# 32x32 block turns on VectorE in place of TensorE transposes, for q and k of two batches and for the late normalised tokens

## The chip, the cores and the metric

The kernel runs on one core of one Trainium2 chip. The metric is the device time of one execution in microseconds (us). Before the change three runs gave a median of 906.98 us, from 904.29 to 907.66.

## The reference

Inputs are float32: q, k and v of shape (4 batches, 8 heads, 768 tokens, 64), a decay per head, and two weights of 512x2048 and 2048x512. First comes causal linear attention with decay, in blocks of the sequence:

```python
intra = einsum('bhij,bhjd->bhid', einsum('bhic,bhjc->bhij', qb, kb) * Dmask, vb)
inter = einsum('bhid,bhde->bhie', qb * lam_pow, kv_state)
out[block] = intra + inter
kv_state = lam_block * kv_state + einsum('bhsd,bhse->bhde', kb * rev_pow, vb)
```

The heads are put side by side into x of (4, 768, 512). Then a Fourier mixing layer with a channel MLP:

```python
u = x + real(fft(fft(x, axis=1), axis=2))
un = (u - mean(u)) / sqrt(var(u) + 1e-6)
out = u + maximum(un @ w_ch1, 0) @ w_ch2
```

Scores need q and k with the head dimension on partitions, and the MLP needs un with the 512 features on partitions. Both arrive with tokens on partitions, so both are transposed.

## The kernel before, in words

**Attention.** A batch b is cut into 6 chunks of 128 tokens (`attn_chunk`). A chunk loads k, q and v, all heads, with tokens on partitions (L261, on SP's queue). TensorE transposes two heads at a time into PSUM (L272 for k, L277 for q, four 128x128 each) and ScalarE copies the result to kT and qT (L274, L279). VectorE scales q into qs (L282), reading it from PSUM. Scores (L290) are masked by the decay on VectorE (L294). The state is updated (L305), the output is summed from state and scores (L318, L322), copied (L325), transposed back (L329) and copied to x (L332, L333). Tokens are also stored to two DRAM arrays xa and xb (L336 to L340, on ScalarE's queue), from which the FFT gathers tokens in mirrored order (L377, L380, L385, on GpSimd's queue).

**Fourier layer.** `fft_ln` folds each batch by its symmetries on VectorE (L365 to L368, L405 to L416), so that the sequence transform is 20 matmuls (L440); the width transform (L453 to L458) follows, and VectorE adds the result to x (L509 to L513). `norm(g)` works on groups of two tiles of 128 tokens: statistics (L470), the factor (L474 and L475 on GpSimd), the normalised tokens un (L482), four TensorE transposes a tile (L486), a ScalarE copy into ut (L487).

**MLP, plain and late.** There are 12 groups (batch, g). The first four are PLAIN: their MLP runs as written (L545, rectified by ScalarE at L553 and VectorE at L551; L559, added and stored at L565, L566). The other eight are LATE: ut is stored to DRAM as utd (L494), u as ud (L497). Two late groups at a time are then multiplied with a seven-product scheme for 2x2 blocks (L627, L674). This needs sums and differences of weight blocks (`combine_weights`, L604) and of the two groups (us, ur, L617 to L620); `load_u` (L611) reads utd back.

**Weights.** 32 raw loads of 512 KB (L227) are converted on VectorE and ScalarE (L232 to L240) in the first 190 us.

**Order.** Each stage is a generator that yields an estimated duration. `weave` interleaves a lead with another generator in a given ratio: weight conversion under the first attention batches, then the plain groups' MLP as fill under the attention and Fourier stages of batches 1 to 3, and what is left of it under `combine_weights`. The Tile scheduler may then move instructions ahead of one another by its own estimates; only those marked `keep_in_program_order` stay. On each engine the instructions then run in a fixed order. Tiles come from pools: a new tile waits until the readers of the one whose buffer it takes have finished. When attention and Fourier stages end, their pools are closed, and the late stage's tiles lie over the same memory.

Of the kernel before, what the change touches and what calls it, by code (L numbers as in the profile page):

```python
# [10 lines left out]
F32 = mybir.dt.float32  # L11
# [64 lines left out]
def kernel(  # L76
# [10 lines left out]
    nc = tc.nc  # L87
    B, H, S, D = q.shape
    DM = H * D
    DFF = moe_w_ch1.shape[1]  # L90
    C = 128
    NC = S // C
    HC = NC // 2
    HP = H // 2
    NK = S // 4 + 1
    KO = DM // 128
# [5 lines left out]
    G = 2  # L102
# [18 lines left out]
    ld = front_pool("ld", 2)  # L121
    at = front_pool("at", 1)
    xn = front_pool("xn", HC)
    fp = front_pool("fp", 1)
# [13 lines left out]
    def new(pool, shape, tag, **kw):  # L138
        cnt[0] += 1
        return pool.tile(shape, F32, tag=tag, name=f"{tag}{cnt[0]}", **kw)  # L140

    def psum_a(shape):
        return new(pa, shape, "pa")
# [12 lines left out]
    n, b2 = 1, 0  # L156
# [45 lines left out]
    def row_of(j, n=128):  # L202
        return bass.IndirectOffsetOnAxis(ap=ix[0:n, j:j + 1], axis=0)
# [45 lines left out]
            yield 1.0  # L249


    xs, xn_, xd = {}, {}, {}

    def pair(t, hp):
        return t[:, 2 * hp:2 * hp + 2, :].rearrange("p a d -> p (a d)")

    def attn_chunk(b, c):
        rows = slice(c * C, (c + 1) * C)
        kt, qt, vt = (new(ld, [C, H, D], nm) for nm in ("k", "q", "v"))
        for t, src in ((kt, k), (qt, q), (vt, v)):  # L260
            nc.sync.dma_start(t, src[b, :, rows, :].rearrange("h p d -> p h d"))  # L261
        if b == 0:
            load_tables(c)

        last = c == NC - 1
        if not last:
            kd = new(at, [C, H, D], "kd")
            nc.gpsimd.tensor_tensor(kd, kt, kpow, op=ALU.mult)

        ptk = psum_a([128, HP, C])  # L270
        for hp in range(HP):
            nc.tensor.transpose(ptk[:, hp, :], pair(kt, hp), ident)  # L272
        kT = new(at, [128, HP, C], "kT", bufs=2)
        nc.scalar.copy(kT, ptk)  # L274
        ptq = psum_a([128, HP, C])
        for hp in range(HP):
            nc.tensor.transpose(ptq[:, hp, :], pair(qt, hp), ident)  # L277
        qT = new(at, [128, HP, C], "qT", bufs=2)
        nc.scalar.copy(qT, ptq)  # L279
        if c > 0:  # L280
            qs = new(at, [128, HP, C], "qs")
            nc.vector.tensor_tensor(qs, ptq, qpow, op=ALU.mult)  # L282
        yield 1.2


        mm = nc.tensor.matmul
        pss = [psum_a([C, HP, C]) for _ in range(2)]
        for hp in range(HP):
            for hi in range(2):
                mm(pss[hi][:, hp, :], lhsT=kT[HD[hi], hp, :], rhs=qT[HD[hi], hp, :], start=True, stop=True)  # L290
        sc = []
        for hi in range(2):
            t = new(at, [C, HP, C], "sc", bufs=3)
            nc.vector.tensor_tensor(t, pss[hi], decay[:, hi::2, :], op=ALU.mult)  # L294
            sc.append(t)
        yield 1.5


        s_old, s_new = st[(c + 1) % 2], st[c % 2]
        if not last:  # L300
            pu = psum_a([128, HP, D])
            for hp in range(HP):
                for hi in range(2):
                    h = 2 * hp + hi
                    mm(pu[HD[hi], hp, :], lhsT=kd[:, h, :], rhs=vt[:, h, :], start=True, stop=True)  # L305
            if c == 0:
                nc.vector.tensor_copy(s_new, pu)
            else:
                nc.gpsimd.tensor_tensor(s_new, s_old, spow.broadcast_to([128, HP, D]), op=ALU.mult)
                nc.vector.tensor_tensor(s_new, s_new, pu, op=ALU.add)  # L310
            yield 0.9


        po = psum_a([128, HP, C])
        if c > 0:
            for hp in range(HP):
                for hi in range(2):
                    mm(po[HD[hi], hp, :], lhsT=s_old[HD[hi], hp, :], rhs=qs[HD[hi], hp, :],  # L318
                       start=(hp == 0), stop=False, skip_group_check=True)
        for hp in range(HP):  # L320
            for hi in range(2):
                mm(po[HD[hi], hp, :], lhsT=vt[:, 2 * hp + hi, :], rhs=sc[hi][:, hp, :],  # L322
                   start=(c == 0 and hp == 0), stop=(hp == HP - 1), skip_group_check=True)
        oT = new(at, [128, HP, C], "oT")
        nc.scalar.copy(oT, po)  # L325
        yield 2.0
        px = psum_a([C, HP, 128])
        for hp in range(HP):
            nc.tensor.transpose(px[:, hp, :], oT[:, hp, :], ident)  # L329
        px = px.rearrange("p h e -> p (h e)")  # L330
        x = xn_[b, c] = new(xp, [C, DM], "x") if c < HC else new(xn, [C, DM], "xn")
        nc.scalar.copy(x[:, 0:HM], px[:, 0:HM])  # L332
        nc.scalar.copy(x[:, HM:DM], px[:, DM - 1:HM - 1:-1])  # L333
        if c == 0:
            xd[b] = (dram.tile([S - 256, DM], F32, name=f"xa{b}"), dram.tile([257, DM], F32, name=f"xb{b}"))
            nc.scalar.dma_start(xd[b][1][256:257], x[0:1])  # L336
        elif c < NC - 1:
            nc.scalar.dma_start(xd[b][0][(c - 1) * C:c * C], x)
        if c >= NC - 2:
            nc.scalar.dma_start(xd[b][1][(c - NC + 2) * C:(c - NC + 3) * C], x)  # L340
        if c == NC - 2:
            mirror_a(b)
        elif c == NC - 1:
            mirror_b(b)
        yield 1.7
# [9 lines left out]
        nc.gpsimd.memset(t, 0.0)  # L355

    gather = nc.gpsimd.indirect_dma_start
    eo, r1s = {}, {}

    def fold_x(b, a, n, i, lo, hi):  # L360

        e, o = eo[b][a]
        tt = nc.vector.tensor_tensor

        tc.keep_in_program_order(tt(e[0:n, i, 0:DM], lo, hi, op=ALU.add))  # L365
        tc.keep_in_program_order(tt(o[0:n, i, 0:DM], lo, hi, op=ALU.subtract))
        tt(e[0:n, i, 1:HM], e[0:n, i, 1:HM], e[0:n, i, HM:DM - 1], op=ALU.add)
        tt(o[0:n, i, 1:HM], o[0:n, i, 1:HM], o[0:n, i, HM:DM - 1], op=ALU.subtract)  # L368

    def mirror_a(b):  # L370

        xa = xd[b][0]
        r1 = r1s[b] = [new(fp, [128, DM], f"r{a}") for a in range(2)]

        eo[b] = [(new(fp, [128, 2, 2 * W], f"fe{a}"), new(fp, [128, 2, 2 * W], f"fo{a}")) for a in range(2)]
        for a, n in enumerate(BLK):
            gather(out=r1[a][0:n], out_offset=None, in_=xa[:, :], in_offset=row_of(a, n))  # L377
        for t in range(2, HC):
            u = xs[b, HC + t] = new(xp, [128, DM], "x")
            gather(out=u[:, :], out_offset=None, in_=xa[:, :], in_offset=row_of(2 + t))  # L380
# [6 lines left out]
            xs[b, t] = xn_.pop((b, t))  # L387

    def fold_a(b):
        r1 = r1s.pop(b)  # L390
        for a, n in enumerate(BLK):
            fold_x(b, a, n, 1, r1[a][0:n], xn_[b, HC + a][0:n])

    def fold_b(b):

# [31 lines left out]
    def fft_ln(b):  # L427
# [38 lines left out]
        def norm(g):  # L466
            mv = new(np_, [128, G, 2], "mv")
            for i in range(G):
                stt = new(np_, [128, 6], "stt")
                nc.vector.bn_stats(stt, xs[b, TT[g][i]])  # L470
                nc.vector.bn_aggr(mv[:, i, :], stt)
            ve = new(np_, [128, G], "ve")
            rs = new(np_, [128, G], "rs")
            nc.gpsimd.tensor_scalar(ve, mv[:, :, 1], EPS, None, op0=ALU.add)  # L474
            nc.gpsimd.tensor_tensor(rs, ve, mhalf, op=ALU.pow)  # L475
            yield 1.0
            ut = new(up, [128, KO, G * 128], "ut")
            for i in range(G):
                un = new(np_, [128, DM], "un", bufs=1)
                u = xs[b, TT[g][i]]  # L480
                for o, x in ((un[:, 0:HM], u[:, 0:HM]), (un[:, HM:DM], u[:, DM - 1:HM - 1:-1])):
                    nc.vector.tensor_scalar(o, x, mv[:, i, 0:1], rs[:, i:i + 1],  # L482
                                            op0=ALU.subtract, op1=ALU.mult)
                pt = psum_a([128, KO, 128])
                for c in range(KO):
                    nc.tensor.transpose(pt[:, c, :], un[:, 128 * c:128 * c + 128], ident)  # L486
                nc.scalar.copy(ut[:, :, 128 * i:128 * i + 128], pt)  # L487
                yield 0.7
            if (b, g) in PLAIN:
                uts[b, g] = ut  # L490
                return

            utd[b, g] = dram.tile([128, KO, G * 128], F32, name=f"utd{b}{g}")
            nc.sync.dma_start(utd[b, g], ut)  # L494
            for T in TT[g]:
                ud[b, T] = dram.tile([128, DM], F32, name=f"ud{b}{T}")
                nc.sync.dma_start(ud[b, T], xs.pop((b, T)))  # L497
# [309 lines left out]
```

## Time and profile before

| | |
|---|---|
| median of 3 runs | 906.98 us (904.29 to 907.66) |
| the profiled execution | 908.43 us, its span 906.4 us |
| mean granted TensorE clock | 0.975 |
| PE busy | 826.5 us, 91% |
| DVE busy | 437.0 us, 48% |
| ACT busy | 209.0 us, 23% |
| POOL busy | 90.7 us, 10% |
| DMA packets | 96190, 72.43 MB, 77536 of them under 512 B |
| k, q, v loads (256 KB each) to landing | 3.8, 3.9, 3.2 us |
| utd stores (512 KB each) to landing | 3.3 us |
| ud stores (256 KB each) to landing | 2.1 us |

PE is TensorE's matmuls, PEld its weight loads, DVE is VectorE, ACT ScalarE, POOL GpSimd, SP the engine that issues most DMAs. In a group's line stand source line, engine, operation, output<-input by name, shapes and count; then the busy time in us and the mean ns of one; then the idle time of the engine just before them and what ended it. A line of the timeline begins with the start and the duration in us; "x4" are so many instructions of one kind in a row. Matmuls are pipelined, so a group's mean ns is longer than the time until the next can start. The slices of the page are 40 equal parts of the span (22.7 us each), with the busy share in tenths.

### The profile page before, as it was taken

Reading aid. Unit: us, or ns where it says so; the run is one execution under the profiler, and the core shown is the slowest. Engines: PE = TensorE matmul, PEld = TensorE weight load, DVE = VectorE, ACT = ScalarE, POOL = GpSimd, SP = SyncE. Lnnn points to the kernel's source line nnn. Section 1 sums busy time; section 2 is a strip of 40 time slices with the busy share of each in tenths; the row PEclk is TensorE's granted clock in tenths of the full one; section 3 lists DMA queues with packets and bytes.
Section 4 is the critical chain, followed back from the end, with each engine's and each line's share of the span. In section 5 each row is a group of like instructions: output and inputs, shape, how many; then the busy total and the mean of one; then the engine's idle time right before and its main releaser. Section 6 shows DMA issues by size and latency. Waiting matters only on the chain.

```text
span 906.4 us, 11761 instructions
## 1 busy us (share of the span) xinstructions
PE 826.5 (91%) x4660; PEld 652.9 (72%) x4660; DVE 437.0 (48%) x1006; ACT 209.0 (23%) x467; POOL 90.7 (10%) x108
## 2 busy tenths in 40 slices
PE   4775678699999999999999899999999999999997
PEld 2564566545865578567874588888888888888886
DVE  4779869854532135443567756115531454135410
ACT  3665436620211212223221021002200120012100
POOL 2214211100010110012200100000000000000000
PEclk9988789899999999999999999999999999999999
DMA  9899316611013241344216001110011100110010
GB/s 230 232 249 252 111 52 179 209 39 35 24 47 93 74 120 47 116 141 129 88 47 215 29 1 47 46 35 12 1 59 47 35 1 1 47 47 1 0 35 24
DMA packets 96190, 72.43 MB, mean 80 GB/s; under 512 B 77536, under 2 KB 79080, under 8 KB 96136
## 3 DMA queue, kind: packets, MB, share of 16 engines
q1 hardware_dynamic: 90176, 57.51, 22.3%
q0 software_dynamic: 2496, 7.87, 2.7%
q10 hardware_dynamic: 3464, 6.30, 2.0%
q8 instruction: 37, 0.61, 0.3%
q14 instruction: 17, 0.14, 0.0%
HBM read 50.68 MB, written 20.99 MB: 79 GB/s over the span
## 4 chain that ended last, share of the span: by engine, by line
PE 51%; DVE 5%; issue 1%; DMA 1%; POOL 1%; ACT 0%; POOLq 0%; DVEq 0%; ACTq 0%
PE p L627 21%; PE p L674 21%; PE pm L545 1%; PE pm L559 1%; PE pa L440 1%; PE pa L486 1%; PE pa L290 1%; PE pa L322 1%; DVE stt L470 1%; DVE w1s L604 1%; DVE w2s L604 1%; PE pa L318 1%; POOL rs L475 0%; DVE x L512 0%; DVE x L513 0%
## 5 line engine op out<-in xcount | busy, mean ns | idle before, releaser
L545 PE MATMUL pm<-ut,w 128*128 128x256 f32 x512 | 124.2, 392 | 10.0 <-ACT hr L553 8.2
L559 PE MATMUL pm<-w,hr 128*128 128x512 f32 x256 | 120.6, 602 | 0.0
L545 PEld LDWEIGHTS pm<-ut,w 128*128 128x128 f32 x512 | 95.9, 194 | 26.3 <-ACT hr L553 8.9
L627 PE MATMUL p<-ur,w 128*128 128x256 f32 x384 | 95.1, 382 | 3.3 <-DVE ur L620 1.9
L627 PEld LDWEIGHTS p<-ur,w 128*128 128x128 f32 x384 | 73.3, 191 | 14.5 <-issue 2.3
L559 PEld LDWEIGHTS pm<-w,hr 128*128 128x128 f32 x256 | 44.8, 190 | 40.3 <-issue 38.8
L627 PE MATMUL p<-us,w1s 128*128 128x256 f32 x256 | 66.6, 383 | 0.0
L674 PE MATMUL p<-w,hs 128*128 128x256 f32 x256 | 58.0, 379 | 0.5 <-DVE y L695 0.5
L674 PE MATMUL p<-w2s,hs 128*128 128x256 f32 x256 | 57.9, 379 | 0.0
L674 PE MATMUL p<-w,ha 128*128 128x256 f32 x256 | 57.9, 379 | 0.0
L535 POOL DMA_INDIRECT out_dram<-y,ix x12 | 13.3, 1109 | 409.9 <-DVE y L698 370.9
L627 PEld LDWEIGHTS p<-us,w1s 128*128 128x128 f32 x256 | 49.2, 192 | 6.9
L674 PEld LDWEIGHTS p<-w,hs 128*128 128x128 f32 x256 | 48.5, 190 | 7.5 <-DVE y L695 0.9
L674 PEld LDWEIGHTS p<-w2s,hs 128*128 128x128 f32 x256 | 48.6, 190 | 6.6
L674 PEld LDWEIGHTS p<-w,ha 128*128 128x128 f32 x256 | 48.6, 190 | 6.6
L290 PEld LDWEIGHTS pa<-qT,kT 64*128 64x128 f32 x384 | 30.1, 193 | 25.9 <-ACT qT L279 14.4
L654 ACT COPY ha<-p 128x256 f32<-128x256 f32 x32 | 11.9, 372 | 155.6 <-PE p L627 155.5
L290 PE MATMUL pa<-qT,kT 64*128 64x128 f32 x384 | 36.2, 291 | 11.7 <-ACT qT L279 10.0
L294 DVE TENSOR_TENSOR sc<-pa,decay 128x512 f32<-128x512 f32 x48 | 31.8, 684 | 29.1 <-PE pa L290 26.3
L322 PE MATMUL pa<-sc,v 128*64 128x128 f32 x384 | 31.2, 290 | 9.8 <-DVE sc L294 9.8
L665 DVE TENSOR_TENSOR ha<-p,ha 128x256 f32<-128x256 f32 x32 | 13.6, 425 | 47.1 <-ACT ha L664 47.1
L322 PEld LDWEIGHTS pa<-sc,v 128*64 128x64 f32 x384 | 23.4, 143 | 17.5 <-DVE sc L294 13.4
(141 smaller groups left out, 1188.3 us busy)
## 6 DMA issues: line engine op xcount, KB each, us to landing
raw<-in_moe_w_ch_dram SPq DMA_DIRECT2D x32, 512.0 KB, 5.2
k<-in_k_dram SPq DMA_DIRECT2D x24, 256.0 KB, 3.8
q<-in_q_dram SPq DMA_DIRECT2D x24, 256.0 KB, 3.9
v<-in_v_dram SPq DMA_DIRECT2D x24, 256.0 KB, 3.2
ud<-x SPq DMA_DIRECT2D x16, 256.0 KB, 2.1
utd<-ut SPq DMA_DIRECT2D x8, 512.0 KB, 3.3
u<-ud SPq DMA_DIRECT2D x16, 256.0 KB, 2.6
ur<-utd SPq DMA_DIRECT2D x8, 512.0 KB, 5.6
```

The lines of the kernel that those rows point to most:

```text
L290: mm(pss[hi][:, hp, :], lhsT=kT[HD[hi], hp, :], rhs=qT[HD[hi], hp, :], start=True, stop=True)
L294: nc.vector.tensor_tensor(t, pss[hi], decay[:, hi::2, :], op=ALU.mult)
L318: mm(po[HD[hi], hp, :], lhsT=s_old[HD[hi], hp, :], rhs=qs[HD[hi], hp, :], start=(hp == 0), stop=False, skip_group_check=True)
L322: mm(po[HD[hi], hp, :], lhsT=vt[:, 2 * hp + hi, :], rhs=sc[hi][:, hp, :], start=(c == 0 and hp == 0), stop=(hp == HP - 1), skip_group_chec ...
L535: nc.gpsimd.indirect_dma_start(out=out.rearrange("b s d -> (b s) d"), out_offset=row_of(2 + HC * (b + 1) + T - HC), in_=y[:, :], in_offset ...
L545: nc.tensor.matmul(ps, lhsT=w1[:, c, 128 * fc:128 * fc + 128], rhs=ut[:, c, :], start=(c == 0), stop=(c == KO - 1))
L559: nc.tensor.matmul(ps, lhsT=hr[fc // 4][:, fc % 4, 128 * i:128 * i + 128], rhs=w2[:, fc, :], start=(fc == 0), stop=(fc == FO - 1))
L604: V.tensor_tensor(o[:, i:i + n // 2], x[:, i:i + n // 2], y[:, i:i + n // 2], op=op)
L627: nc.tensor.matmul(ps, lhsT=s2.A[a][:, kt, 128 * i:128 * i + 128], rhs=U[b][:, kt, :], start=(first and kt == 0), stop=(kt == 1), skip_gro ...
L654: nc.scalar.copy(a11, two(X))
L665: V.tensor_tensor(a22, two(Z), a22, op=ADD)
L674: nc.tensor.matmul(ps, lhsT=h[a][:, s, i, :], rhs=s2.B[b][:, i, :], start=(first and i == 0), stop=(i == HF - 1), skip_group_check=True)
```

## The change

Four things change; line numbers in the diff's new code differ from those above.

1. For batches 2 and 3, kT and qT no longer come from TensorE. Every second chunk, `turned` fills a tile for two chunks (kb or qb, one buffer each) with 16 DMAs. A DMA takes 32 of a head's 64 dimensions for 256 tokens and puts 32x32 blocks where they belong after a transpose, each still unturned: 32 partitions, 8 runs of 32 elements (128 B) each. VectorE's transpose, which turns each 32x32 block in place, then makes kT or qT of a chunk from it. k with tokens on partitions is still loaded for the state, except in the last chunk. qs reads qT in SBUF.
2. For batches 0 and 1, q is loaded into the memory of qb and kb by turns.
3. For late groups, un is turned in 32x32 blocks by VectorE into uq (one buffer), and four DMAs a tile write the blocks to their places in utd, in runs of 128 B. The plain groups keep TensorE's transposes.
4. The first gather of a batch lands in a half of the tile fo, and the fold works on it in place; the tiles r0 and r1 are gone.

```diff
+        def turned(nm, load, src):
+            if c % 2 == 0:
+                t = qk[load] = new(ld, [128, HP, 2 * C], load, bufs=1)
+                for a in range(4):
+                    for hp in range(HP):
+                        nc.sync.dma_start(t[32 * a:32 * a + 32, hp].rearrange("n (t d) -> n t d", d=32),
+                                          src[b, 2 * hp + a // 2, c * C:(c + 2) * C, 32 * (a % 2):32 * (a % 2) + 32]
+                                          .rearrange("(t n) d -> n t d", n=32))
+            tT = new(at, [128, HP, C], nm, bufs=2)
+            nc.vector.transpose(tT, qk[load][:, :, c % 2 * C:(c % 2 + 1) * C])
+            return tT
+
+        blocks = b >= 2
+        if blocks:
+            kT, qT = turned("kT", "kb", k), turned("qT", "qb", q)
+            ptq = qT
+            if not last:
+                kt = natural("k", k)
+        else:
+            kt, qt = natural("k", k), new(ld, [128, HP, 2 * C], "kb" if c % 2 else "qb", bufs=1)
...
-        r1 = r1s[b] = [new(fp, [128, DM], f"r{a}") for a in range(2)]
-            gather(out=r1[a][0:n], out_offset=None, in_=xa[:, :], in_offset=row_of(a, n))
+            gather(out=eo[b][a][1][0:n, 1, 0:DM], out_offset=None, in_=xa[:, :], in_offset=row_of(a, n))
...
-                pt = psum_a([128, KO, 128])
-                for c in range(KO):
-                    nc.tensor.transpose(pt[:, c, :], un[:, 128 * c:128 * c + 128], ident)
-                nc.scalar.copy(ut[:, :, 128 * i:128 * i + 128], pt)
+                if plain:
...
+                else:
+                    uq = new(np_, [128, DM], "uq", bufs=1)
+                    nc.vector.transpose(uq, un)
+                    for r in range(0, 128, 32):
+                        dst = to[:, :, 128 * i + r:128 * i + r + 32].rearrange("(a d) c n -> d c a n", d=32)
+                        src = uq[r:r + 32].rearrange("p (c a n) -> p c a n", c=KO, n=32)
+                        nc.sync.dma_start(dst, src)
...
-            nc.sync.dma_start(utd[b, g], ut)
```

More of the change, by code (lines that the diff above doesn't have):

```diff
@@ L249, in weights @@
             yield 1.0
-    xs, xn_, xd = {}, {}, {}
+    xs, xn_, xd, qk = {}, {}, {}, {}
     def pair(t, hp):
@@ L258, in attn_chunk, with natural @@
         rows = slice(c * C, (c + 1) * C)
-        kt, qt, vt = (new(ld, [C, H, D], nm) for nm in ("k", "q", "v"))
-        for t, src in ((kt, k), (qt, q), (vt, v)):
+        last = c == NC - 1
+        def natural(nm, src):
+            t = new(ld, [C, H, D], nm)
             nc.sync.dma_start(t, src[b, :, rows, :].rearrange("h p d -> p h d"))
+            return t
+        def turned(nm, load, src):
[17 more added lines that the diff above has]
+            kt, qt = natural("k", k), new(ld, [128, HP, 2 * C], "kb" if c % 2 else "qb", bufs=1)
+            qt = qt[:, 0:2].rearrange("p a (b d) -> p (a b) d", d=D)
+            nc.sync.dma_start(qt, q[b, :, rows, :].rearrange("h p d -> p h d"))
+        vt = natural("v", v)
         if b == 0:
             load_tables(c)
-        last = c == NC - 1
         if not last:
@@ L268, in attn_chunk @@
             nc.gpsimd.tensor_tensor(kd, kt, kpow, op=ALU.mult)
[L270 to L279, printed above, removed]
+        if not blocks:
+            ptk = psum_a([128, HP, C])
+            for hp in range(HP):
+                nc.tensor.transpose(ptk[:, hp, :], pair(kt, hp), ident)
+            kT = new(at, [128, HP, C], "kT", bufs=2)
+            nc.scalar.copy(kT, ptk)
+            ptq = psum_a([128, HP, C])
+            for hp in range(HP):
+                nc.tensor.transpose(ptq[:, hp, :], pair(qt, hp), ident)
+            qT = new(at, [128, HP, C], "qT", bufs=2)
+            nc.scalar.copy(qT, ptq)
         if c > 0:
@@ L357 @@
     gather = nc.gpsimd.indirect_dma_start
-    eo, r1s = {}, {}
+    eo = {}
     def fold_x(b, a, n, i, lo, hi):
@@ L389, in fold_a @@
     def fold_a(b):
-        r1 = r1s.pop(b)
         for a, n in enumerate(BLK):
-            fold_x(b, a, n, 1, r1[a][0:n], xn_[b, HC + a][0:n])
+            fold_x(b, a, n, 1, eo[b][a][1][0:n, 1, 0:DM], xn_[b, HC + a][0:n])
     def fold_b(b):
@@ L476, in norm @@
             yield 1.0
-            ut = new(up, [128, KO, G * 128], "ut")
+            plain = (b, g) in PLAIN
+            if plain:
+                ut = uts[b, g] = new(up, [128, KO, G * 128], "ut")
+            else:
+                to = utd[b, g] = dram.tile([128, KO, G * 128], F32, name=f"utd{b}{g}")
             for i in range(G):
@@ L483, in norm @@
                                             op0=ALU.subtract, op1=ALU.mult)
-                pt = psum_a([128, KO, 128])
-                for c in range(KO):
-                    nc.tensor.transpose(pt[:, c, :], un[:, 128 * c:128 * c + 128], ident)
-                nc.scalar.copy(ut[:, :, 128 * i:128 * i + 128], pt)
+                if plain:
+                    pt = psum_a([128, KO, 128])
+                    for c in range(KO):
+                        nc.tensor.transpose(pt[:, c, :], un[:, 128 * c:128 * c + 128], ident)
+                    nc.scalar.copy(ut[:, :, 128 * i:128 * i + 128], pt)
+                else:
+                    uq = new(np_, [128, DM], "uq", bufs=1)
[4 more added lines that the diff above has]
+                        nc.sync.dma_start(dst, src)
                 yield 0.7
-            if (b, g) in PLAIN:
-                uts[b, g] = ut
+            if plain:
                 return
-            utd[b, g] = dram.tile([128, KO, G * 128], F32, name=f"utd{b}{g}")
-            nc.sync.dma_start(utd[b, g], ut)
             for T in TT[g]:
```

## The prediction

> **What bounds the kernel now.** I read the page's busy shares first, then the slices, then the chain that ended last, then the groups with shapes apart, then the timeline around the last attention chunk. Shares, slices and chain from the page:
>
> ```profile
> PE 826.5 (91%) x4660; PEld 652.9 (72%) x4660; DVE 437.0 (48%) x1006; ACT 209.0 (23%) x467; POOL 90.7 (10%) x108
> ...
> PE   4775678699999999999999899999999999999997
> ...
> PE 51%; DVE 5%; issue 1%; DMA 1%; POOL 1%; ACT 0%; POOLq 0%; DVEq 0%; ACTq 0%
> ```
>
> PE is full from slice 9 (about 204 us) to the end. From 513 us on, the chain is PE L627 and L674 alone (384 us of the four late pieces); of the compute in it the change touches only the start. So the question is when the first late matmuls can run.
>
> The groups that the change removes or halves, shapes apart (busy, mean ns | idle before, releaser):
>
> ```profile
> L272 PE MATMUL pa<-ident,k 128*128 128x128 f32 x96 | 16.3, 295 | 4.5 <-DMA k<-in_k_dram 4.5
> L277 PE MATMUL pa<-ident,q 128*128 128x128 f32 x96 | 16.0, 293 | 0.0
> L486 PE MATMUL pa<-ident,un 128*128 128x128 f32 x96 | 16.7, 294 | 13.2 <-DVE un L482 13.2
> ```
>
> The 290 ns are latency. What a transpose costs the stream is its pitch; timeline of PE's weight loads around 403 us:
>
> ```profile
> 402.98 0.47 PEld L272 LDWEIGHTS pa<-ident,k 128*128 128x128 f32 x4
> ...
> 403.42 0.47 PEld L277 LDWEIGHTS pa<-ident,q 128*128 128x128 f32 x4
> ```
>
> Four transposes take 0.44 us, 0.11 each. The other pitches, read the same way: L545 0.43 and L559 0.86 a matmul (two instructions each); L290 1.09 us for a chunk when its two head halves alternate, 2.16 when they are issued apart.
>
> Then the end of attention and the start of late (timeline):
>
> ```profile
> 443.12 0.60 PE L329 MATMUL pa<-ident,oT 128*128 128x128 f32 x4
> ...
> 450.37 0.69 DVE L365 TENSOR_TENSOR fe<-x,x 128x512 f32<-128x512 f32 x1 [1.44 <-DMA x<-xb,ix]
> ...
> 491.58 2.36 DVE L604 TENSOR_TENSOR w1s<-w 128x1024 f32<-128x1024 f32 x2 [0.56 <-PE pa L486]
> ...
> 513.14 1.22 PE L627 MATMUL p<-ur,w 128*128 128x256 f32 x2 [1.87 <-DVE ur L620]
> ```
>
> Behind the last attention transposes stands a serial chain of 70 us: store, gather, fold (L365), FFT, widths, norms, combine_weights (L604, 16 of 128x1024 at a pitch of 1.135 us), first late matmul. PE isn't idle in it because the plain groups' MLP (L545, L559) fills it.
>
> **The Trainium skill.** "VectorE: DVE Perf Modes", The three transpose paths: VectorE turns 32x32 blocks alone, SBUF to SBUF; 128x128 bf16 311 ns there, 390 ns on TensorE. No turn is in this trace; TensorE's 295 ns agrees as a latency, and the pitch of 0.11 is what counts. "DMA: Bandwidth & Descriptors", Anatomy of one DMA (SWDGE path): about 2 us fixed, mostly the write's receipt; the trace agrees for stores from SP too (ud lands in 2.1 us). Same page, Specifications: runs under 512 B lose rate, small writes being read, changed and written back. No run of before has 128 B runs; q and k with 256 B land in 3.8 us. "TensorE: Matmul & The Clock Gate", Architectural detail: "ACT/DVE are strict FIFO". So a VectorE turn that waits for a store holds all behind it; among DVE's waits of before none is for a store, so this trace shows no case.
>
> **The change, part by part.**
>
> *Removed from PE.* q and k of two batches: 12 chunks x 8 = 96 transposes, 10.6 us. Late norms: 8 groups x 8 = 64, 7.0 us. In the changed order L290 alternates its halves in five chunks of b=2 more: 5 x 1.08 = 5.4 us. In all 23 us. ACT loses 40 copies of 0.59 us; ACT is 23% busy, worth nothing by itself.
>
> *Added on DVE.* 24 turns of q and k, 16 of norms, each 128x512. Lower bound 0.5 us (a 128x512 pass at the best pitch seen), upper 1.2 (a 128x1024 pass), taken 0.6, the pitch of a 128x512 pass such as L365. 24 us on an engine with 48% busy; hidden by PE except where DVE leads, in the tail (3 turns, 1.8 us).
>
> *Added on SP.* 192 block loads (32 KB) and 64 block stores (64 KB), less 14 q and k loads and 8 utd stores. Issues stand 0.46 us apart, and each DMA waits for the eighth before it: 0.46 us each while landing stays under 3.7 us. A pair's 32 loads take 15 us plus 2; the changed order has 36 us of fill ahead of the pairs, so hidden, up to about 1.1 us per load. The uq stores stand between block loads on SP and wait for their turn on DVE, so loads of b=3 queue behind b=2's norms; also inside that cover. In the weight stage (145 to 190 us) 32 of the loads stand between raw loads, and DVE paces conversions there (40.4 of 45 us busy): 4 turns, 2.4 us, and some late raw: +3, from 0 to +10.
>
> *Moved: fill.* This decides. The plain groups have 256 matmuls of L545 (0.43 us each) and 128 of L559 (0.86), each shown as two instructions. Counted in the order of both programs: before, 43 L545 and 32 L559 still stand behind the last attention transposes, 18.5 + 27.5 = 46.0 us. In the changed order only 8 L559 do, 6.9 us. 39.1 us of fill have moved ahead of b=3's last chunks (85 matmuls before chunks 2 and 3, 25 before 4 and 5), to cover block loads and turns.
>
> *Last attention transposes.* From 443.1: +39.1 fill; -10.6 q and k; -4.4 norms (five of the late groups lie ahead of this point, 40 transposes); -5.4 L290; +3 weight stage; PE's waits between 209 and 443 us sum to about 17 us, and those behind ACT's qT copies and un (10.0 and 13.2 us over the kernel in the groups) partly go: -4. Sum +17.7: 460.8.
>
> *The tail.* +7.25 to the gathered x (443.12 to 450.37): 468.1. +15.0 through fold, FFT and first width (450.37 to 465.3): 483.1. +15.7 DVE's norms as they stand in the new order, to the start of L604: 498.8. Then 16 x 1.135 = 18.2, turns 1.8, un 2.2, us and ur 2.5: 523.5 for the operands of late. PE has 6.9 us of fill for about 60 us, so it mostly stands.
>
> *A wait added.* uq has one buffer: each turn waits for the four stores of the turn before, 3 x 0.46 + 2.1 = 3.5 us, plus 0.6 for itself. The last two turns (g=0) stand behind us and ur on DVE, and late's first ACT copy (ha11) waits for the last stores, since its tile lies over uq. Queued behind: ACT's copies, then DVE's additions, then PE when the 8 banks are full, 17 matmuls (7.3 us) into late. The last stores land about 10.2 us after ur: 10.2 - 7.3 = +2.9. Bounds: 0 (landing as for 32 KB) to +10 (each hop twice as long).
>
> *Sum.* Late's work is effectively started at 523.5 + 2.9 = 526.4. Before it was 513.14 less the 4 matmuls already done (1.7): 511.4. **+15.0 us**. The profiled execution has 908.43 (span 906.4), 1.5 above the median of 906.98; I add to the median: 922.
>
> *Gathers in place.* The first gather lands in fo instead of r0 and r1: no instruction more. It must wait for the last reader of fo, the FFT of the batch before, a chunk or more earlier; hidden by attention, and at worst one gather (4.4 us) late in each batch.
>
> **Rivals.**
>
> *A, not slower: PE's waits go.* If turned operands are there early, the 13 us of waits that I leave in 209 to 443 vanish, since kT and qT no longer come through PE, PSUM and ACT. For it: L290 waited 10.0 us for ACT's qT. Against: half of this is b=0 and 1, and waits for sc, oT and un stay. It decides when at most 2.5 us of the 13 are left: then 922 - 10.5 = 911.5, the edge of what can be told from no change; all gone and the uq wait nothing: 922 - 13 - 2.9 = 906. Faster needs nil weight stage as well: 903.
>
> *B: block loads bind SP.* If a load of 128 B runs costs 2 us of queue instead of 0.46, a pair costs 64 us against 36 of fill: +28 for b=3's worst pair, less the overlap with fill that is then in the tail; the weight stage +20. 950 to 970. For it: 49,152 runs of 128 B (192 x 256) more in loads and 32,768 (64 x 512) in stores, on 96,190 packets of before. Against: 256 B packets take 15 to 18 ns of an engine, so 256 of them over 16 engines are 0.3 us. At 1.1 us each only the weight stage shows: +7, 929.
>
> *C: DVE in order.* Turns waiting for stores hold hr evacuations (L551) that PE's MLP needs: per late group one hop of 3.5 us, at most 8 x 3.5 = 28 less what pm's three banks cover; half exposed gives +14: 936. For it: strict order and one buffer. Against: other DVE work stands between the turns.
>
> *D: fill does not matter,* the tail is bound by DVE either way. Then the +17.7 is wrong only if the chain ahead of the last transposes isn't PE's; slices of 9 there say it is.
>
> **Chances.** Main (912 to 930) 0.63; B or C, up to 970, 0.22; A 0.12, of which 0.04 really faster; else 0.03. A measurement of this kernel tells about 0.5% (4.5 us) from no change. Faster 0.04, same 0.09, slower 0.87. The range leaves out about 0.1 at each end: 910 to 946.
>
> **What would show it.** Right: last attention transposes near 461; PE's slices between 465 and 525 falling to 1 to 5; L627 first delayed by DVE's ur, then by ACT's ha waiting on uq's stores; late unchanged at 384 us. Turn 0.6 us, block load at a pitch of 0.46. Wrong: a busy tail (fill left over), block loads at 1 us or more with L290 waiting for DVE turns of kT and qT, or the last transposes before 450.

## The result, and the profile after

The changed kernel takes 933.76 us (median of 4 runs, 929.43 to 941.74), the kernel before beside it 907.32 us. The ratio is 1.0303, 95% interval 1.0223 to 1.0384: 26.4 us slower. The profiled execution took 929.43 us against 908.43 of before, +21.0.

The page of the changed kernel, shares, slices and chain:

```profile
PE 811.6 (87%) x4500; PEld 642.6 (69%) x4500; DVE 460.2 (50%) x1046; ACT 187.0 (20%) x427; POOL 86.8 (9%) x108
...
PE   4766688699999989999972289999999999999997
...
PE 70%; DVE 14%; DMA 7%; issue 4%; ACT 1%; POOL 1%; SPq 1%; POOLq 0%; DVEq 0%; ACTq 0%
```

160 TensorE transposes are gone, and PE has 14.9 us less to do. But the slices have a hole that before has not: 7, 2, 2, 8 from 464 us on (a slice is 23.2 us). The chain's shares can't be set against those of before (DVE 5%, DMA 1%): there the chain is followed back only to 370.08 us, here to the first 20 us, so it takes in the stages that load and convert weights.

PE's timeline around the hole:

```profile
464.20 0.60 PE L357 MATMUL pa<-ident,oT 128*128 128x128 f32 x4
464.63 7.03 PE L595 MATMUL pm<-w,hr 128*128 128x512 f32 x16
476.39 1.63 PE L466 MATMUL pa<-cs,fe 128*128 128x193 f32 x4 [4.72 <-DVE fe L435]
...
504.67 3.75 PE L663 MATMUL p<-ur,w 128*128 128x256 f32 x8 [14.48 <-DMA ur<-utd]
527.02 8.24 PE L663 MATMUL p<-ur,w 128*128 128x256 f32 x24 [18.59 <-DVE ur L656]
539.44 4.97 PE L663 MATMUL p<-us,w1s 128*128 128x256 f32 x14 [4.18 <-ACT ha L690]
```

Behind the last attention transposes (464.20) stand 8 matmuls of fill (7.03 us), then PE waits: 4.7 us for the fold, 14.5 for ur from DRAM, 18.6 for DVE's ur, 4.2 for ScalarE's copy. From 539.44 on the late stage runs as before: to the end of the span 388 us, before it was 393 from 513.14, when 12 matmuls (5.2 us) fewer were done.

Where the fill went, PE between chunks 1 and 2 of batch 3:

```profile
370.62 0.60 PE L357 MATMUL pa<-ident,oT 128*128 128x128 f32 x4
371.06 27.63 PE L595 MATMUL pm<-w,hr 128*128 128x512 f32 x64
398.53 23.04 PE L581 MATMUL pm<-ut,w 128*128 128x256 f32 x106
421.50 1.16 PE L318 MATMUL pa<-qT,kT 64*128 64x128 f32 x16
```

50.4 us of fill in one piece. And SP's queue while it runs (start, duration, operation, count):

```profile
371.89 2.73 SPq L527 DMA_DIRECT2D utd<-uq  x4
374.67 2.10 SPq L272 DMA_DIRECT2D kb<-in_k_dram  x4
377.12 2.59 SPq L527 DMA_DIRECT2D utd<-uq  x4
379.76 2.10 SPq L272 DMA_DIRECT2D kb<-in_k_dram  x4
386.40 2.59 SPq L527 DMA_DIRECT2D utd<-uq  x4
389.04 2.10 SPq L272 DMA_DIRECT2D qb<-in_q_dram  x4
391.49 2.59 SPq L527 DMA_DIRECT2D utd<-uq  x4
394.12 6.05 SPq L272 DMA_DIRECT2D qb<-in_q_dram  x12
```

The 32 loads of batch 3's second pair of chunks start at 350.77 and end at 400.17, 49.4 us: 17.7 for the loads, 15.7 for the 24 uq stores of batch 2 between them, 4.3 for ud stores with their waits, and 11.7 in which SP issues nothing. A uq store can't be issued before its turn on DVE. Sixteen loads of the pair behind took 9.8 us with nothing between; but the first kb loads of batch 3 took 23.7, also with no store between:

```profile
298.00 23.68 SPq L272 DMA_DIRECT2D kb<-in_k_dram  x16
...
403.09 9.80 SPq L272 DMA_DIRECT2D kb<-in_k_dram  x16
```

The waits of SP (us in all, times, longest) name what held them, beside what held the uq stores:

```profile
SPq L272 <- DMA xa<-xn: 31.2, 3, 15.6
SPq L527 <- DVE uq L523: 27.5, 12, 6.5
```

The first line is a wait that block loads need for no data: xa is the attention output, which ScalarE's queue stores. A DMA waits for an earlier one (the prediction's "eighth before it"), and by this line that can be one of another queue. Which of these waits is the cause, or only what one sees beside it, is what the experiments ask.

### The profile page after: what moved, and what is told of

Same layout as the page of the kernel before. It is cut to its first block, busy times and chain, and to the rows that moved or that the text cites. A ratio compares the mean times of both kernels' runs of the same rounds, so it can differ in the third digit from the quotient of the medians.

```text
span 927.7 us, 11691 instructions
## 1 busy us (share of the span) xinstructions
PE 811.6 (87%) x4500; PEld 642.6 (69%) x4500; DVE 460.2 (50%) x1046; ACT 187.0 (20%) x427; POOL 86.8 (9%) x108
## 4 chain that ended last, share of the span: by engine, by line
PE 70%; DVE 14%; DMA 7%; issue 4%; ACT 1%; POOL 1%; SPq 1%; POOLq 0%; DVEq 0%; ACTq 0%
PE p L710 21%; PE p L663 20%; PE pm L595 10%; PE pm L581 7%; PE pa L466 3%; PE pa L350 2%; DMA raw<-in_moe_w_ch_dram 2%; PE pa L318 2%; PE pa L346 1%; DMA utd<-uq 1%; DMA x<-xb,ix 1%; DVE w L239 1%; DVE pw L235 1%; PE pa L357 1%; PE pa L333 1%
## 5 line engine op out<-in xcount | busy, mean ns | idle before, releaser
L581 PE MATMUL pm<-ut,w 128*128 128x256 f32 x512 | 126.5, 397 | 10.8 <-ACT hr L589 8.8
L663 PE MATMUL p<-ur,w 128*128 128x256 f32 x384 | 98.2, 394 | 33.1 <-DVE ur L656 18.6
L581 PEld LDWEIGHTS pm<-ut,w 128*128 128x128 f32 x512 | 97.1, 196 | 30.0 <-ACT hr L589 9.8
L595 PE MATMUL pm<-w,hr 128*128 128x512 f32 x256 | 113.0, 598 | 0.0
L663 PEld LDWEIGHTS p<-ur,w 128*128 128x128 f32 x384 | 75.9, 198 | 45.1 <-DVE ur L656 19.3
L595 PEld LDWEIGHTS pm<-w,hr 128*128 128x128 f32 x256 | 48.5, 192 | 57.8 <-issue 57.4
L690 ACT COPY ha<-p 128x256 f32<-128x256 f32 x32 | 11.7, 373 | 181.9 <-PE p L663 138.4
L350 PE MATMUL pa<-sc,v 128*64 128x128 f32 x384 | 33.0, 291 | 13.3 <-DVE sc L322 13.3
L318 PE MATMUL pa<-qT,kT 64*128 64x128 f32 x384 | 32.3, 304 | 9.8 <-ACT qT L307 9.8
L295 POOL TENSOR_TENSOR kd<-k,decay 128x512 f32<-128x512 f32 x20 | 22.8, 1142 | 188.8 <-DMA k<-in_k_dram 111.9
L350 PEld LDWEIGHTS pa<-sc,v 128*64 128x64 f32 x384 | 24.1, 142 | 21.7 <-DVE sc L322 15.7
L318 PEld LDWEIGHTS pa<-qT,kT 64*128 64x128 f32 x384 | 27.0, 204 | 16.5 <-ACT qT L307 12.5
```

Of the source, the lines that this page charges most:

```text
L581: nc.tensor.matmul(ps, lhsT=w1[:, c, 128 * fc:128 * fc + 128], rhs=ut[:, c, :], start=(c == 0), stop=(c == KO - 1))
L595: nc.tensor.matmul(ps, lhsT=hr[fc // 4][:, fc % 4, 128 * i:128 * i + 128], rhs=w2[:, fc, :], start=(fc == 0), stop=(fc == FO - 1))
L663: nc.tensor.matmul(ps, lhsT=s2.A[a][:, kt, 128 * i:128 * i + 128], rhs=U[b][:, kt, :], start=(first and kt == 0), stop=(kt == 1), skip_gro ...
L690: nc.scalar.copy(a11, two(X))
```

## The experiments

**The two parts apart.** Theory F: the loss is the fill spent ahead of the tail. Rival S: loads and turns are dear by themselves. First q and k alone are changed, with late norms transposed as before (parts of the edit):

```diff
-                    uq = new(np_, [128, DM], "uq", bufs=1)
-                    nc.vector.transpose(uq, un)
...
+                pt = psum_a([128, KO, 128])
+                for c in range(KO):
+                    nc.tensor.transpose(pt[:, c, :], un[:, 128 * c:128 * c + 128], ident)
+                nc.scalar.copy(ut[:, :, 128 * i:128 * i + 128], pt)
...
+            nc.sync.dma_start(utd[b, g], ut)
```

> The change of q and k alone (norms by TensorE as before). Theory F (the loss is fill spent ahead of the tail): here 36 matmuls of L581's kind and 32 of L595's (43 us) still stand behind the last attention transposes, nearly as before (46 us), so the tail stays covered; 96 transposes (10.6 us) go, the weight stage costs +4: 897 to 904 us. Rival S (block loads on SP and turns on DVE are dear by themselves, whatever the fill): a good half of the measured +26 stays: 917 or more.

Measured 904.58 us (before beside it 910.31), ratio 0.9941, 0.9916 to 0.9966. S falls for this part; F's value is just missed: the first FFT matmul of batch 1 stands at 218.13 us in its profile, against 209.53 before, so the weight stage took 8.6 of the 10.6 us saved, not 4. (In the profiles of kernels without block loads this point lies at 208.35 to 212.71, so some us of it vary by themselves.) Then the late norms alone:

```diff
-        blocks = b >= 2
+        blocks = False
```

> The change of the late norms alone (q and k by TensorE as before). F: 64 and 47 matmuls of fill (68 us) are left for the tail, more than before; 64 transposes (7.0 us) go, the wait of the last uq stores adds at most 4: 900 to 907 us. S: the 64 stores and 16 turns cost by themselves: 915 or more.

Measured 884.57 us, ratio 0.9727, 0.9691 to 0.9764: 25.7 us faster, where at most 10 were expected. PE's timeline at the start of late:

```profile
443.91 15.81 PE L581 MATMUL pm<-ut,w 128*128 128x256 f32 x72
459.56 27.63 PE L595 MATMUL pm<-w,hr 128*128 128x512 f32 x64
487.02 6.52 PE L663 MATMUL p<-ur,w 128*128 128x256 f32 x28
```

PE goes from the last width straight through 43 us of fill into late, 24.4 us earlier than the 511.4 of before. Adding PE's start-to-start times by line from batch 1's first FFT matmul on, the scores took 13.3 us instead of 19.6 (both halves alternate everywhere) and waits 6.5 instead of 9.9; with the 7.0 us of transposes and the 1.2 us earlier start this is 18 of 24 us. Another 3.2 us lie in L559's pitch, 0.91 us a matmul before and 0.88 here. The rest I haven't attributed.

So the parts apart give -5.7 and -25.7, together they give +26.4. Neither is dear: counted like this, 58 us lie in their meeting. Both kernels also have parts 2 and 4 of the change (q's buffer, the gathers in place), which no run tests by themselves; what these gain or lose is in both numbers, so the 58 is not exact, and the 25.7 may not be the turns' alone.

**Fill, tried from both sides.** In the kernel before, fill was moved forward:

```diff
-    run(weave(fr, back, (len(PLAIN) * t_mlp - FO * 1.7 - 25.0) / t_rest))
+    run(weave(fr, back, (len(PLAIN) * t_mlp - FO * 1.7 - -40.0) / t_rest))
```

> The kernel before, with a reserve of fill of -40 instead of 25 in the last weave, so that only 16 matmuls of L559 (13.8 us) are left behind the last attention transposes: 32 us of fill moved forward, nothing else changed. F: the tail stands without cover, and +18 to +28 follow: 925 to 935 us. S: fill order alone is worth little: 904 to 912.

Measured 946.98 us, ratio 1.0397, 1.0356 to 1.0439: +36.7, more than forecast. PE in this kernel's tail (start, duration, line, and idle time ahead):

```profile
507.74 1.09 PE L486 MATMUL pa<-ident,un 128*128 128x128 f32 x4 [5.79 <-DVE un L482]
...
533.38 3.75 PE L627 MATMUL p<-ur,w 128*128 128x256 f32 x8 [1.47 <-DMA ur<-utd]
551.87 2.05 PE L627 MATMUL p<-us,w1s 128*128 128x256 f32 x4 [14.74 <-DVE us L618]
```

An uncovered tail, here with TensorE's transposes in it, costs more than the change does, with no block load or turn in the kernel. Then the fill of the changed kernel was held in program order, for the last two plain groups at the first matmul of each sum (L581) and at every fourth (L595):

```diff
+                if (b, g) in PLAIN[2:] and c == 0:
+                    tc.keep_in_program_order(mm)
...
+                if (b, g) in PLAIN[2:] and fc % 4 == 0:
+                    tc.keep_in_program_order(mm)
```

> The whole change, and the first matmul of each sum of the last two plain groups kept in program order, so that 64 and 48 matmuls of fill (69 us) are left behind the last attention transposes. F: PE's saving of 23 us comes through, less 4 for the weight stage and some waiting for turns and for uq's stores: 886 to 900 us. S: as with the change, 928 to 940.

Measured 935.77 us, ratio 1.0255, 1.0187 to 1.0323: no gain, and F as I had put it falls. The tail is covered here (PE is busy for all of 500 to 550 us), but the hole has moved. PE and DVE at batch 3's second pair:

```profile
408.42 2.08 PE L318 MATMUL pa<-qT,kT 64*128 64x128 f32 x16 [19.46 <-DVE qT L276]
```

```profile
396.25 1.30 DVE L276 STREAM_TRANSPOSE kT<-kb 128x512 f32<-128x512 f32 x2
407.56 1.30 DVE L276 STREAM_TRANSPOSE qT<-qb 128x512 f32<-128x512 f32 x2 [10.01 <-DMA qb<-in_q_dram]
```

Between 300 and 450 us PE is idle for 44 us. Of these 21.7 are waits for qT, whose loads come late; 13.4 are a wait for batch 2's fold (L466, at 335.25), which held fill no longer covers, and 5.8 one for DVE's masked scores. So the fill had been hiding a real lateness of the loads, about half of what is seen here; the rest is what held fill no longer covers. Fill is only where the price is paid. So a new theory, I: loads and stores meet on SP, which issues in order; the loads come late, and either fill or idle time pays. Rival L: runs of 128 B are slow to load, wherever they are issued.

**Parting loads and stores.** One queue changed in each:

```diff
-                        nc.sync.dma_start(dst, src)
+                        nc.scalar.dma_start(dst, src)
```

> The whole change, but the 64 stores of uq are issued from ScalarE's queue, so that block loads on SP no longer stand behind stores that wait for turns. 64 and 44 matmuls of fill are left for the tail. Theory I (the loss is the meeting of both parts on SP: loads behind stores, and fill burnt to cover them): PE's 23 us come through, 870 to 888 us. Rival L (runs of 128 B are slow to load whatever stands between): PE waits for qT as with fill held, 905 or more.

```diff
-                        nc.sync.dma_start(t[32 * a:32 * a + 32, hp].rearrange("n (t d) -> n t d", d=32),
+                        nc.scalar.dma_start(t[32 * a:32 * a + 32, hp].rearrange("n (t d) -> n t d", d=32),
```

> The whole change, but the 192 block loads are issued from ScalarE's queue and the uq stores stay on SP. 64 and 46 matmuls of fill are left. I: 870 to 890 us, a little more than with the stores moved if ScalarE's copies wait behind loads. L: 905 or more.

Stores moved: 886.62 us, ratio 0.9774, 0.9722 to 0.9826. Loads moved: 879.36 us, 0.9684, 0.9632 to 0.9735, 54 us below the change. L falls: the DMAs are the same 256, only the queue is another. kb's loads in the profile with the loads moved (ns of an issue, least, median and longest; first and last start in us):

```profile
L272 ACTq DMA_DIRECT2D kb<-in_k_dram x96: 317/461/1626, 165.3 to 376.4; - x96
```

A load still costs 0.46 us of its queue (median). kb's last is issued at 376 us instead of 412. Moving the queue also changed the scheduler's order: 64 and 46 matmuls of fill are left for the tail. So these two runs show the meeting as a whole, its lateness and its fill. The held kernel has 64 and 48 left, nearly the same, and stands beside it: between 300 and 450 us PE is idle for 5.5 us with the loads moved, against 44, and not at all for qT. kb, qb and uq have one buffer each in both, so these alone don't make the loss. What stays open is how it divides on SP between the uq stores and the waits for xa: with the stores moved, loads waited 6.4 us for xa instead of 31.2, so that went too.

**One batch only, on either queue.**

```diff
-        blocks = b >= 2
+        blocks = b == 2
```

> The late norms turned, and q and k by blocks for batch 2 alone: batch 2's first loads come before any uq store, batch 3 has none. 64 matmuls of L581's kind and 37 of L595's are left. I: 48 transposes less than with the norms alone (5.3 us), the weight stage +4: 880 to 890. L: 895 or more.

Measured 887.35 us, ratio 0.9793, 0.9729 to 0.9856. Then batch 3 alone (`b == 3`), on SP and on ScalarE's queue:

> The late norms turned, and q and k by blocks for batch 3 alone, all on SP: only the loads that stand behind batch 2's uq stores. 11 matmuls of L581's kind and 26 of L595's (27 us) are left for the tail. I: the meeting on SP alone makes it dearer than with batch 2 alone (887 us): 895 to 915. If it's any block loads that cost, and not their place: 880 to 890, as with batch 2.

> As the one before, but batch 3's loads are issued from ScalarE's queue. 64 matmuls and 47 are left. I: 870 to 882 us: the norms' gain (884.6 with them alone) and 48 transposes (5.3 us) less, with no block loads in the weight stage. If place on SP doesn't matter: as the one before.

On SP 908.18 us, ratio 0.9987, 0.9966 to 1.0008. On ScalarE's queue 882.96 us, 0.9681, 0.9626 to 0.9737 (a shade above the 882 I had set as its upper end). The same 96 loads, with the fill that the scheduler then burns for them, cost 25 us more on SP, where they stand behind batch 2's stores; their waits for xa are 8.0 us there. (By its trace 11 and 32 matmuls of fill are left for the tail.) With batch 2 alone only six loads stand between stores; its 48 transposes fewer gain nothing over the norms alone (884.57), but no loss of this size is seen. SP in the kernel with batch 3 on SP:

```profile
355.30 3.29 SPq L272 DMA_DIRECT2D qb<-in_q_dram  x4
358.68 3.64 SPq L527 DMA_DIRECT2D utd<-uq  x4
362.37 2.11 SPq L272 DMA_DIRECT2D qb<-in_q_dram  x4
369.38 2.59 SPq L527 DMA_DIRECT2D utd<-uq  x4
```

Four loads, then four stores that wait for a turn, as in the changed kernel.

**The wait for uq's last stores.** Batch 3's norms were transposed by TensorE again, with the rest of the change kept (`late_b` is `b == 3`):

```diff
-            if plain:
+            turn_pe = plain or (late_b)
+            if turn_pe:
```

> The whole change, but the norms of batch 3 are transposed by TensorE and stored whole as before, so that no uq store is left in the tail; fill order as with the change (8 matmuls left). The wait of late's first ScalarE copy for uq's stores (4.2 us of PE idle in the trace, and some 3 us of slower first matmuls) goes: 5 to 9 us below the change, 924 to 929. If uq's stores cost nothing there: 932 or more.

Measured 941.78 us (ratio 1.0351, 1.0283 to 1.0418): not better, a miss. Removing the wait brought another order into the tail. PE there:

```profile
502.56 1.08 PE L520 MATMUL pa<-ident,un 128*128 128x128 f32 x4 [5.79 <-DVE un L515]
...
504.16 1.12 PE L520 MATMUL pa<-ident,un 128*128 128x128 f32 x4 [0.51 <-DVE un L515]
505.06 0.64 PE L480 MATMUL pa<-dt,ys 128*128 128x128 f32 x2
...
518.26 0.38 PE L483 MATMUL pa<-dt,ys 128*1 128x128 f32 x2
```

The next width (L480) stands behind the transposes on PE, and these wait for un; so norms and widths go in turn, and the last width begins at 518.26 us, 49.9 us after the last attention transposes (468.36). In the changed kernel, where DVE turns, the last is at 489.81, 25.6 after. In this pair of kernels the turns in the tail gain at least what the wait costs; the intervals of the two totals overlap (1.0283 to 1.0418, and 1.0223 to 1.0384), so more is not shown.

With PE covered (loads on ScalarE's queue), the same exchange:

> Loads from ScalarE's queue, and the norms of batch 3 transposed by TensorE again. PE is full in the tail here, so 48 transposes (5.3 us) come back on the path: 881 to 890. If the turns' stores were the tail's limit instead: 872 to 878.

Measured 885.59 us, ratio 0.972, 0.9678 to 0.9763: 6.2 us more than with the turns. The value is in the range forecast, but not for the reason given: batch 3's norms are 24 transposes, not 48. PE's start-to-start times give them 2.8 us, and 1.2 us more are waits. The rest isn't attributed.

**The loads split over both queues** (batch 2's on SP, batch 3's on ScalarE's):

> The whole change with batch 2's block loads on SP and batch 3's on ScalarE's queue. 64 matmuls and 37 are left. I: batch 2 as with norms and batch 2 alone (887), 48 transposes less (5.3): 876 to 886. If any block load on SP harms, as with batch 3 alone: 900 or more.

Measured 889.64 us, ratio 0.9754, 0.9706 to 0.9803, from 883.36 to 894.9: between the two expectations. Batch 3's loads don't harm, but why it stays 10 us above loads moved as a whole isn't settled.

The best version is thus the change with its block loads on ScalarE's queue: 879.36 us, 54 us below the change and 28.5 below before. Most of this comes with the late norms: without any block load the kernel takes 884.57 us, and the ratios' intervals overlap (0.9632 to 0.9735, and 0.9691 to 0.9764). In the two profiles batch 1's FFT starts at 215.79 us with the loads and at 208.35 without, which takes 7.4 of the 10.6 us that 96 transposes save.

## Why the prediction was right or wrong

Right in sign and range (910 to 946), too small in size: +15.0 against +26.4 by medians, +21.0 by profiles.

The range held because the order was counted from the two programs, which have the fill moved whatever the reason, and not because the loads' lateness was seen.

- **The order, and last attention transposes.** Forecast 460.8, measured 464.20. The weight stage was +3.8 (first FFT matmul of batch 1 at 213.34 against 209.53), forecast +3. The term that failed is the -4 for PE's waits, out of "about 17 us". From batch 1's FFT to this point (stretch, its length, PE busy) the windows show, before and after:

```profile
209.53:443.12 233.59, 228.24 (x1487) 0.99 0.29 84
213.34:464.20 250.86, 245.36 (x1485) 0.99 0.38 82
```

PE was idle for 5.35 us before and is for 5.50 after: there was little to save, and nothing was saved. L290's 10.0 us of waits for qT lie ahead of this stretch. Rival A, which counted on 13 us of waits here, had 5.35 to win. In the other direction, the 67 matmuls moved ahead took 36.1 us by start-to-start times, where 39.1 were forecast.
- **The tail.** Gathered x at 472.92 (forecast 468.1), first L640 at 502.58 (498.8), operands of late at 526.96 (523.5): the steps behind the transposes took 62.8 us against 62.7 forecast.
- **The wait added.** Forecast +2.9. The chain of the changed kernel has the hops:

```profile
526.53 2.21 DMA utd<-uq
531.56 2.22 DMA utd<-uq
536.60 2.20 DMA utd<-uq
```

A hop, from store to store, is 5.0 us, not 4.1: a store of 128 B runs holds SP for 0.62 us, not 0.46. ScalarE's copy waited until the last landed, PE stood 4.18 us. The 12 matmuls ahead of that took 8.24 us instead of 5.2, which the forecast had at nothing. With the four done at 504.67, 16 were done by 539.44, which is worth 6.9 us at the usual pitch: late effectively started at 532.5 instead of 526.4. Against 511.4 that is +21.1, which is the profiled difference.
- **The step that was mis-sized** is thus two terms of the sum: 3.4 us ahead of the tail, where the -4 for waits did not come, and 2.7 in the uq wait, 5.6 instead of 2.9: 4.2 of idle time and 3.1 of slower matmuls, less 1.7 for the four done early. The other 5 us are between the profiled execution and the median: of the four runs the profiled one is the fastest. The rest have a lower mean granted clock (0.939 to 0.944, against 0.949 here and 0.975 before). That they lose it in the hole is likely, where the windows of the profiled run show 0.58 to 0.68, but no run's trace shows it.
- **The step that was wrong in its reason** is "also inside that cover", of block loads behind uq stores. I took the fill as moved once for all and the loads as hidden. The runs show that the loads' place on SP, with the stores, is why the fill goes ahead: held back, it is replaced by idle time, half of it for qT (935.77); parted, the kernel is 28.5 us faster than before. "0.46 us each while landing stays under 3.7 us" failed in the same place: by the trace a kb load stood for up to 15.6 us until an xa store of ScalarE's queue had landed. Of rival B the place on SP was right and the price per load wrong (0.45 to 0.46 us by median, not 2).
- **Turns on DVE:** a pitch of 0.6 us was assumed, and it was right: two in a row take 1.30 us, one by itself 0.70 to 0.71 (a 128x512 pass 0.68 to 0.69), so the second starts 0.60 us after the first. Rival C's waits are small: uq's turns waited 12.6 us in all for stores.
- **PE's saving of 23 us**: with the loads moved the kernel gains 28.5 us; how much of this is those 23 was not measured apart. One piece is: L290 took 5.4 us less from batch 1's FFT to the last attention transposes, as forecast.

The Trainium skill, "DMA: Bandwidth & Descriptors", Issuing engines are not separate DMA queues, says that issuing from several engines saves only the issuing sequencer's time, usually small. Here that time, with the waits in it, was the price: 49.4 us until 32 loads were issued, of which the loads themselves are 17.7, and 25 us of the kernel's time between batch 3's loads on SP and on ScalarE's queue.

## What to carry to other kernels

Before a second stream of small DMAs goes on a queue, ask what each DMA ahead of it waits for, and which DMA of another queue it may itself stand behind: on SP here, loads that were ready got the waits of stores that were not. Fill that hides such lateness is spent once, so count what is left of it where a serial chain needs it, and try the parts of a change alone before judging any of them.

## What the runs showed of the hardware

In the changed kernel stores of 64 KB in runs of 128 B to DRAM landed in 2.2 us (median), loads of 32 KB in such runs in 2.0 and 2.1 (up to 2.6 in other runs); ud's stores of 256 KB took 2.1. At the issue a store held SP for 0.62 us, a load for 0.45 (medians).

The granted clock fell in the hole. Of each window: length, busy time of PE, PEld, DVE, ACT and POOL, then the clock, and DMA share and GB/s:

```profile
504.60:527.00 22.40, 3.75 (x8) 2.53 (x8) 22.36 (x27) 0.00 (x0) 0.00 (x0) 0.58 0.48 123
527.00:539.40 12.40, 8.24 (x24) 6.45 (x24) 2.16 (x4) 0.39 (x2) 0.00 (x0) 0.77 0.43 75
```

The 12 matmuls at 527.02, behind 18.6 us without one, took 0.69 us each instead of 0.43.
